# Four matmuls to a weight load in a cached-attention decode kernel: K in groups of eight pairs with the transposes by halves of the head, V in four PSUM banks for two pairs, w_down behind the last K

## Chip, cores, metric

One core of a Trainium2 chip runs the kernel. The metric is the device time of one execution in microseconds (us). All runs told here are of the state "fast"; the program has one core, so there is no second die to disturb it.

## The reference, cut to what matters

```python
# A_: attention of one new token against a cache; B_: a gated MLP on the same batch (its own w_gate, w_up, w_down)
x: (4, 1, 1024)   k_cache, v_cache: (4, 32, 8192, 128)   wq: (1024, 4096)   wo: (4096, 1024)     # all bf16
q = (x @ wq) per head;  p = softmax(q . k_cache / sqrt(128));  o = p . v_cache;  a = o @ wo
b = x + sigmoid(r) * ((silu(x @ w_gate) * (x @ w_up)) @ w_down)          # w_*: 1024 x 3584 and 3584 x 1024
out = g * a + (1 - g) * b
```

The two caches are 537 MB, everything together 575.7 MB, read once.

## The kernel before

K and V are walked in 32 *pairs* (four heads of one batch row, 8 MB of K or of V each; the name is the program's, for two ring slots of 4 MB). A ring of five slots in SBUF takes all large loads in program order. For K, VectorE (DVE) transposes 32x32 blocks of 32-bit words and TensorE (PE) multiplies by a shifted copy of q, so that all scores of a group of pairs collect in one PSUM tile. After a group comes a softmax; then V of the group is multiplied by the weights, a pair of V after each pair of K. At the end several V pairs follow each other without K between them, and the blocks of w_o come last.

```python
CJ = 32; JT = 4; RD = 8; GD = 4        # 8 transposes a pair, 4 pairs a group
LAG = GD                               # V runs one group behind K
ring = const.tile([P, NS, RING], BF)   # NS = 5 slots of 4 MB
...
def k_pair(d):
    ks = load_pair(kv_view(A_k_cache, d), RING)
    for n in range(RD):
        nc.vector.transpose(out=flat_t, in_=kn[:, c * CJ * Dh:(c + 1) * CJ * Dh])           # 128x2048 words
        for he in range(4):
            for z in range(2):                                                              # 2 matmuls a load
                nc.tensor.matmul(sps[:, z, :], lhsT=Z[:, he, s:s + P], rhs=T[:, 16*z:16*z+16, half, :, e], ...)
        ...
def v_pair(d):
    for c, z, w:                                                                            # cut
        for e in range(2):                                                                  # 2 matmuls a load
            nc.tensor.matmul(o_ps[row:row + NM, e, :], lhsT=PB[:, RD * t + c, z, w], rhs=vn[...], ...)
    if t < GD - 1:
        return
    nc.scalar.activation(out=o_sb, in_=o_ps[:, 0, :], func=ACT.Copy, scale=mE[:, 0:1])       # "OS": once in 4 pairs
    nc.vector.scalar_tensor_tensor(out=o_sb, in0=o_ps[:, 1, :], scalar=mE[:, 1:2], in1=o_sb, ...)
    ...                                   # later: 4 small matmuls pick the rest out of o_sb
...
last = [wo_block(g) for g in range(2, NWB - 2)] + ...   # w_o: blocks 0, 1 before the last V pair, 2 to 7 behind it
last.pop(0)()                             # block 2
flush(); flush_late()                     # the last OS goes through its small matmuls
last.pop(0)()                             # block 3
o_rows(GE, NWB)                           # rows of w_o blocks 4 to 7 (GE = 4)
for use in last: use()
```

## Time and profile before

| | before |
|---|---|
| time, median of the first 3 runs (range) | 1343.87 us (1343.86 to 1344.13) |
| PE, DVE busy | 77%, 46% |
| weight loads of K and V | 2048, about 206 us, beside the matmuls |
| DMA | 575.69 MB, 99.5% busy, 429 GB/s |

The page of the kernel before, busy us of each engine (share of the span) and number of instructions. Besides PE and DVE it names PEld (PE's weight loads), ACT (ScalarE) and POOL (GpSimd); SP, further down, is the engine that issues most DMAs:

```profile
PE 1032.8 (77%) x4552; PEld 227.9 (17%) x2364; DVE 614.4 (46%) x369; ACT 50.6 (4%) x46; POOL 62.8 (5%) x161
```

The DMA view of the kernel before: totals, the large queue (packets, MB, share of 16 engines' span), and two lines of the issue table (size of one DMA, median us from issue to landing; the second group, with no size, holds several sizes).

```profile
DMA packets 14316, 576.18 MB, mean 429 GB/s; under 512 B 1598, under 2 KB 1606, under 8 KB 2252
q1 hardware_dynamic: 14276, 575.69, 99.5%
...
ring<-in_A_k_cache_dram SPq DMA_DIRECT2D x14, 4096.0 KB, 34.1
...
ring<-in_A_k_cache_dram SPq DMA_DIRECT2D x25, 36.2
```

The loads are nearly never idle. The issue table says how much is queued ahead: a DMA that takes much longer from issue to landing than its own bytes need stands behind others.

The groups of instructions of the kernel before (busy us, mean ns of one, then the idle time before them and what ended it): transposes, weight loads of K and V, and the two instructions of the OS step.

```profile
L436 DVE STREAM_TRANSPOSE TB<-ring 128x2048 uint32<-128x2048 uint32 x256 | 566.9, 2277 | 492.4 <-DMA ring<-in_A_k_cache_dram 491.5 <-PE S_ps L442 0.8
L442 PEld LDWEIGHTS <-Z 128*128 128x128 bf16 x1024 | 105.4, 103 | 628.0 <-issue 626.4
L513 PEld LDWEIGHTS <-PB 128*32 128x32 bf16 x1024 | 100.7, 98 | 405.1 <-issue 393.7 <-POOL PB L486 5.2 <-POOL Z L421 0.9
L526 DVE SCALAR_TENSOR_TENSOR OS<-o_ps,mE,OS 128x512 f32<-128x512 f32 x8 | 6.0, 751 | 72.2 <-ACT OS L525 72.2
L525 ACT ACTIVATE OS<-o_ps,mE 128x512 f32<-128x512 f32 x8 | 5.5, 687 | 162.8 <-PE o_ps L513 162.8
```

The chain that ended last, in order of time, for the last 82 us of the kernel before (start us, us, what). It goes from V's matmuls back onto the DMA: from 1290 us the end waits for data.

```profile
1260.90 2.81 PE o_ps L513 x8
1263.71 1.82 PE small L533 x8
1265.53 24.73 PE o_ps L513 x112
...
1290.27 30.99 DMA ring<-in_A_v_cache_dram
...
1321.33 16.11 DMA ring<-in_A_wo_dram
...
1337.47 1.90 PE acc L273 x8
```

At 1260.90 the fourth last V pair (pair 28) begins. From there to the end of the span (1342.2) are 81.3 us (*stretch from pair 28 on*).

### The profile page before, as it was taken

Reading aid. Unit: us, or ns where it says so; the run is one execution under the profiler, and the core shown is the slowest. Engines: PE = TensorE matmul, PEld = TensorE weight load, DVE = VectorE, ACT = ScalarE, POOL = GpSimd, SP = SyncE. Lnnn points to the kernel's source line nnn. Section 1 sums busy time; section 2 is a strip of 40 time slices with the busy share of each in tenths; the row PEclk is TensorE's granted clock in tenths of the full one; section 3 lists DMA queues with packets and bytes.
Section 4 is the critical chain, followed back from the end, with each engine's and each line's share of the span. In section 5 each row is a group of like instructions: output and inputs, shape, how many; then the busy total and the mean of one; then the engine's idle time right before and its main releaser. Section 6 shows DMA issues by size and latency. Waiting matters only on the chain.

```text
span 1342.2 us, 7696 instructions
## 1 busy us (share of the span) xinstructions
PE 1032.8 (77%) x4552; PEld 227.9 (17%) x2364; DVE 614.4 (46%) x369; ACT 50.6 (4%) x46; POOL 62.8 (5%) x161
## 2 busy tenths in 40 slices
PE   2565878787788687778977779597778679877898
PEld 0111111111111121111211112111111112111221
DVE  2555655545336554335455556046555254556000
ACT  0000100001000010001000010000100010000100
POOL 2000100001000010001000010000100010000100
PEclk9787988888998888889988889888889899888899
DMA  9999999999999999999999999999999999999997
GB/s 414 436 432 431 439 434 427 445 430 422 445 424 430 442 432 426 438 434 428 438 436 426 432 430 434 436 433 438 428 423 436 430 431 442 436 419 444 419 425 325
DMA packets 14316, 576.18 MB, mean 429 GB/s; under 512 B 1598, under 2 KB 1606, under 8 KB 2252
## 3 DMA queue, kind: packets, MB, share of 16 engines
q1 hardware_dynamic: 14276, 575.69, 99.5%
q8 instruction: 27, 0.44, 0.1%
q14 instruction: 5, 0.04, 0.0%
q10 hardware_dynamic: 8, 0.00, 0.0%
HBM read 575.68 MB, written 0.01 MB: 429 GB/s over the span
## 4 chain that ended last, share of the span: by engine, by line
DMA 66%; DVE 21%; PE 11%; another core or an unknown queue 1%; ACT 0%; issue 0%; SPq 0%; DVEq 0%
DMA ring<-in_A_k_cache_dram 58%; DVE TB L436 21%; PE o_ps L513 9%; DMA ring<-in_A_v_cache_dram 5%; DMA x<-in_gate_w_dram 2%; DMA ring<-in_A_wo_dram 1%; PE S_ps L442 1%; ACT PB L484 0%; PE S_ps L307 0%; PE acc L307 0%; PE acc L273 0%; PE small L533 0%; ACT OS L525 0%; PE small L472 0%
## 5 line engine op out<-in xcount | busy, mean ns | idle before, releaser
L436 DVE STREAM_TRANSPOSE TB<-ring 128x2048 uint32<-128x2048 uint32 x256 | 566.9, 2277 | 492.4 <-DMA ring<-in_A_k_cache_dram 491.5
L442 PE MATMUL S_ps<-TB,Z 128*128 128x512 bf16 x2048 | 518.8, 408 | 219.4 <-DVE TB L436 218.9
L513 PE MATMUL o_ps<-ring,PB 128*32 128x512 bf16 x2048 | 461.4, 388 | 52.6 <-DMA ring<-in_A_v_cache_dram 48.1
L442 PEld LDWEIGHTS <-Z 128*128 128x128 bf16 x1024 | 105.4, 103 | 628.0 <-issue 626.4
L513 PEld LDWEIGHTS <-PB 128*32 128x32 bf16 x1024 | 100.7, 98 | 405.1 <-issue 393.7
L421 POOL COPY Z<-qa 32x4 bf16<-32x4 bf16 x128 | 25.6, 200 | 761.6 <-PE S_ps L442 736.0
L486 POOL COPY PB<-PT 32x1024 bf16<-32x1024 bf16 x16 | 30.3, 1892 | 430.3 <-PE o_ps L513 426.2
L467 ACT ACTIVATE PTs<-S_ps,mx 128x1024 bf16<-128x1024 f32 x8 | 8.9, 1114 | 1020.9 <-DVE mx L463 1020.9
L526 DVE SCALAR_TENSOR_TENSOR OS<-o_ps,mE,OS 128x512 f32<-128x512 f32 x8 | 6.0, 751 | 72.2 <-ACT OS L525 72.2
L484 ACT COPY PB<-PT 32x1024 bf16<-32x1024 bf16 x16 | 30.5, 1908 | 1.5 <-DVE PT L469 1.3
L474 DVE RECIPROCAL rinv<-small 128x16 f32<-128x16 f32 x8 | 2.1, 258 | 42.0 <-PE small L472 42.0
L370 DVE CAST LT<-small 128x64 bf16<-128x64 f32 x2 | 0.4, 224 | 42.3 <-PE small L368 42.3
L236 PE MATMUL small<-identb,x 6*128 6x6 bf16 x8 | 0.6, 195 | 22.3 <-DMA x<-in_gate_w_dram 22.3
L457 DVE TENSOR_REDUCE mx<-S_ps 128x1 f32<-128x1024 f32 x8 | 9.8, 1225 | 15.9 <-PE S_ps L442 15.9
L273 PE MATMUL acc<-ring,LT 128*4 128x512 bf16 x64 | 14.8, 379 | 1.7 <-DMA ring<-in_A_wo_dram 1.0
L469 DVE STREAM_TRANSPOSE PT<-PTs 128x1024 bf16<-128x1024 bf16 x8 | 10.0, 1245 | 10.2 <-ACT PTs L467 10.2
L273 PE MATMUL acc<-ring,hT 128*4 128x512 bf16 x56 | 12.2, 379 | 0.0
L525 ACT ACTIVATE OS<-o_ps,mE 128x512 f32<-128x512 f32 x8 | 5.5, 687 | 162.8 <-PE o_ps L513 162.8
L307 PE MATMUL o_ps<-ring,xw 128*4 128x512 bf16 x56 | 5.7, 536 | 5.3 <-DMA ring<-in_B_w_gate_dram 5.3
L533 PEld LDWEIGHTS small<-selg,OS 128*128 128x128 f32 x64 | 9.0, 208 | 4.1 <-issue 3.9
L533 PE MATMUL small<-selg,OS 128*128 128x16 f32 x64 | 8.7, 269 | 0.0
L238 DVE COPY xw<-small 128x48 bf16<-128x48 bf16 x1 | 0.2, 181 | 15.9 <-PE small L236 15.9
(64 smaller groups left out, 67.2 us busy)
## 6 DMA issues: line engine op xcount, KB each, us to landing
ring<-in_A_k_cache_dram SPq DMA_DIRECT2D x14, 4096.0 KB, 34.1
ring<-in_A_v_cache_dram SPq DMA_DIRECT2D x14, 4096.0 KB, 31.4
ring<-in_B_w_gate_dram SPq DMA_DIRECT2D x1, 7168.0 KB, 37.1
ring<-in_B_w_up_dram SPq DMA_DIRECT2D x1, 7168.0 KB, 39.2
ring<-in_B_w_down_dram SPq DMA_DIRECT2D x2, 3584.0 KB, 27.4
ring<-in_A_wo_dram SPq DMA_DIRECT2D x6, 1024.0 KB, 24.7
ring<-in_A_v_cache_dram SPq DMA_DIRECT2D x2, 2048.0 KB, 28.7
ring<-in_A_v_cache_dram SPq DMA_DIRECT2D x4, 1024.0 KB, 24.7
```

The source lines that it names most:

```text
L273: nc.tensor.matmul(out_ap, lhsT=lhsT, rhs=rhs, start=start, stop=True, skip_group_check=True)
L421: nc.gpsimd.tensor_copy(out=Z[at, :, QP - 1 + QP * q], in_=qa[at, :, h0 + q, b])
L436: nc.vector.transpose(out=flat_t.bitcast(U32), in_=kn[:, c * CJ * Dh:(c + 1) * CJ * Dh].bitcast(U32))
L442: nc.tensor.matmul(sps[:, z, :], lhsT=Z[:, he, s:s + P], rhs=T[:, 16 * z:16 * z + 16, half, :, e], start=(t == 0 and n == 0 and he == 0), ...
L457: nc.vector.tensor_reduce(out=mx[:, 0:1], in_=sps[:].rearrange("p z n -> p (z n)"), axis=AX.X, op=ALU.max)
L467: nc.scalar.activation(out=PTs[:], in_=sps[:].rearrange("p z n -> p (z n)"), func=ACT.Exp, bias=negm[:, 0:1], scale=scale, accum_out=rs[:, ...
L469: nc.vector.transpose(out=PT[:].rearrange("p j i -> p (j i)"), in_=PTs[:])
L484: nc.scalar.copy(out=Bv[at, :, :, q, :], in_=Pv[at])
L486: nc.gpsimd.tensor_copy(out=Bv[at, :, :, q, :], in_=Pv[at])
L513: nc.tensor.matmul(o_ps[row:row + NM, e, :], lhsT=PB[:, RD * t + c, z, w].rearrange("p e s j -> p (e s j)"), rhs=vn[:, j0 * Dh:(j0 + 4) * ...
L526: nc.vector.scalar_tensor_tensor(out=o_sb[:], in0=o_ps[:, 1, :], scalar=mE[:, 1:2], in1=o_sb[:], op0=ALU.mult, op1=ALU.add)
L533: nc.tensor.matmul(oT[:, :], lhsT=o_sb[:, q * Dh:(q + 1) * Dh], rhs=selg[:, q].rearrange("p t s -> p (t s)"), start=(q == 0), stop=(q == 3))
```

## The change

Its intent: a weight load for every four matmuls, no longer for every two. For K, a transpose takes 64 rows of one half of the head (strided input), so that four PSUM banks are filled from one load; the group has eight pairs. For V, four banks collect two pairs. K and V now take four banks each, and the program leaves none for anything else: the diff drops the pool of small tiles and the accumulator of two banks. Three things follow. The small results share banks. w_down, which collected in its own banks from early on, moves behind the last K. And V's banks have to be emptied after every second pair by a new step, the *sums*: a multiply by a mask (`own` in the code) out of PSUM and a reduction of 16 parts on DVE (16 times, in place of the OS step 8 times).

```diff
-    CJ = 32
+    CJ = 64                                # RD = 4, GD = 8
+    GV = 2
 ...                                       # k_pair
-            nc.vector.transpose(out=flat_t.bitcast(U32), in_=kn[:, c * CJ * Dh:(c + 1) * CJ * Dh].bitcast(U32))
-            for he in range(4):
-                for z in range(2):
+            for half in range(2):
+                nc.vector.transpose(out=..., in_=kn[:, half].bitcast(U32))
+                for e in range(2):
+                    for z in range(4):
+                        nc.tensor.matmul(sps[:, z, :], lhsT=Z[:, 2 * half + e, s:s + P], rhs=T[:, 16 * z:16 * z + 16, :, e], ...)
+                step = 2 * n + half
+                if step == 1:
+                    flush_sums()
 ...                                       # v_pair
+        flush_sums()
 ...
+        for u in range(4 * RD):
+            for w in range(4):
+                nc.tensor.matmul(o_ps[row:row + NM, w, :], lhsT=PB[:, ...], rhs=vn[...], ...)
 ...
-        nc.scalar.activation(out=o_sb[:], in_=o_ps[:, 0, :], func=ACT.Copy, scale=mE[:, 0:1])
-        nc.vector.scalar_tensor_tensor(out=o_sb[:], in0=o_ps[:, 1, :], ...)
+        def sums():
+            kept = turned(P, 16 * Dh, F32)
+            nc.vector.tensor_tensor(out=kept..., in0=o_ps[:]..., in1=own[:]..., op=ALU.mult)
+            nc.vector.tensor_reduce(out=OS[:], in_=kept.rearrange("p (k d) -> p d k", d=Dh), axis=AX.X, op=ALU.add)
+        full.append(sums)
 ...                                       # order of work
-    side = {1: lambda: (gu_piece(B_w_up, 1), h_done()), GD - 1: wd_piece}
+    side = {1: lambda: (gu_piece(B_w_up, 1), h_done())}
+            if d == ND - 1:
+                A_ps.append(scp.tile([P, 4, NB], F32, name="S_ps"))
+                wd_piece()
+                add_x()
 ...                                       # after the last V pair: blocks 2, 3, the last sums, 4, rows of 6 and 7, 5, 6, 7
+    flush_sums()
```

## The prediction

> **What bounds the kernel now.** DMA. The page's queue table: 575.69 MB on one queue, busy for 99.5% of the span, mean 429 GB/s. In stretches of 10 us the DMA share is about 1 from the first on (never under 0.89) and falls only in the last 10 us. The Trainium skill, "DMA: Bandwidth & Descriptors", Specifications, gives a ceiling of 435 GB/s; this trace's 429, head and tail included, is 98.6% of it. At 435 the bytes need 1323 us (estimate from that page), so no change to compute can take off more than some 12 us. Compute is behind the data: PE is busy 77%, DVE 46%; K's transposes were preceded by 491.5 us of idle ended by DMA. A K pair takes 36.2 us from issue to landing (issue table), though its 8 MB move in about 19.5 us: some 17 us of other data is still queued ahead, so a consumer may be about that late before the queue runs dry.
>
> **What the change removes.** Half the weight loads of K and V: 1024 of 2048, at 103 and 98 ns, about 103 us of PEld. They are hidden already: in V stretches of the chain 64 matmuls take 13.93 us, 217 ns each, with a load for every second one. The skill, "TensorE: Matmul & The Clock Gate", on LDWEIGHTS, says that loads are pulled ahead of running matmuls; the trace agrees. A few ns per matmul at most come back, and PE is not the limit. Matmuls and their columns stay, and so do the 256 transposes of 2277 ns, if the strided input costs no more.
>
> **What it adds and moves.** Sixteen pairs of DVE instructions (multiply 128x2048 out of PSUM, reduce 128x2048) for eight ACT/DVE pairs of 0.69 + 0.75 us. From the trace's 1.22 us per 1024 elements I estimate 2.3 us each, 74 us in all; DVE busy goes from 614 to about 680 us. A delay of 4.6 us every second pair is inside 17 us. The softmax is half as often and twice as wide, a stall of some 8 us, also inside. The first stretch becomes eight K pairs without V; DVE needs 17.66 us per pair against 19.5 of DMA. w_down (7 MB, 12.2 us of PE) moves to the end, where V needs 14 us of PE per 19.5 us of DMA.
>
> **The tail.** After the last V piece (1325.7 us) the OS step takes 3.2 us longer, but its rows are needed two w_o blocks (3.8 us) later. The end is still the last w_o landing (1337.4), 1.9 us of matmuls, a copy and the store: -1 to +3 us.
>
> **Predicted time:** 1344.5 us; 8 in 10 between 1340.5 and 1348.5. Faster by over 2%: 0.01; within 2%: 0.95; slower by over 2%: 0.04.
>
> **What would show it.** PEld instructions of K and V halve, PEld busy falls by some 100 us; DVE rises by 60 to 80 us; the mean rate stays at 428 to 431 GB/s, the DMA share about 1 in every stretch; the chain still goes back mostly through DMA.
>
> **What would make it wrong.** K transposes well over 2.45 us each through the strided input (the K stretch would starve the queue); a strided reduction of twice my 2.3 us (+2 us in the tail); matmuls waiting for the shared PSUM banks so long that slots come free over 17 us late; a DMA share clearly under 1 mid-run.

## The result, and the profile after

| | before | after |
|---|---|---|
| median of 6 runs (range) | 1343.88 us (1343.76 to 1344.14) | 1349.70 us (1346.55 to 1352.53) |
| ratio, 95% interval | | 1.0042 (1.0029 to 1.0055) |
| granted clock of the profiled run | 0.902 | 0.903 |
| stretch from pair 28 on | 81.3 us | 85.8 us |
| last w_o piece landed, from the span's start | 1338.7 us | 1343.0 us |
| span | 1342.2 us | 1350.4 us |

A ratio is the mean time of one kernel's fast runs over that of the other's of the same rounds, so not quite the ratio of the medians. The change is slower by 0.4%, clear of the noise, within 2%, and outside the range predicted. The profiled run is the slowest of the six.

The page and then the DMA view, after:

```profile
PE 1060.8 (79%) x4512; PEld 128.6 (10%) x1300; DVE 697.8 (52%) x370; ACT 44.5 (3%) x30; POOL 62.8 (5%) x161
```

```profile
DMA packets 14311, 576.10 MB, mean 427 GB/s; under 512 B 1598, under 2 KB 1606, under 8 KB 2252
q1 hardware_dynamic: 14276, 575.69, 99.2%
...
ring<-in_A_k_cache_dram SPq DMA_DIRECT2D x14, 4096.0 KB, 29.8
```

The groups after. Loads are halved, transposes unchanged, and the sums are new:

```profile
L454 DVE STREAM_TRANSPOSE TB<-ring 128x2048 uint32<-128x2048 uint32 x256 | 568.1, 2278 | 436.4 <-DMA ring<-in_A_k_cache_dram 415.2 <-PE S_ps L457 21.2
L548 DVE TENSOR_REDUCE OS<-TB 128x128 f32<-128x2048 f32 x16 | 57.9, 3618 | 0.5
L529 PEld LDWEIGHTS <-PB 128*64 128x64 bf16 x512 | 57.5, 112 | 432.4 <-issue 420.1 <-POOL PB L502 10.9 <-DMA ring<-in_A_v_cache_dram 0.9
L457 PEld LDWEIGHTS <-Z 128*128 128x128 bf16 x512 | 53.7, 105 | 684.0 <-issue 684.0
L546 DVE TENSOR_TENSOR TB<-o_ps,own 128x2048 f32<-128x2048 f32 x16 | 36.3, 2267 | 133.5 <-PE o_ps L529 133.4
```

The weight-load time fell by 99 us and bought nothing on PE: 64 matmuls of V take 13.93 us before (a load for every second one) and 13.93 us after (for every fourth). The reduction costs 3.62 us, where 2.3 had been estimated.

The chain that ended last, after, from pair 28 on. The DMA is gone from it; PE, the multiply (TB L546), the reduction (OS L548) and PE again follow each other to the end.

```profile
1264.61 3.59 PE o_ps L529 x8
...
1268.73 25.17 PE o_ps L529 x120
...
1293.92 2.30 DVE TB L546
...
1296.24 3.63 DVE OS L548
...
1300.51 13.77 PE o_ps L529 x56
...
1318.57 13.95 PE o_ps L529 x64
...
1332.53 2.30 DVE TB L546
...
1334.86 3.62 DVE OS L548
...
1341.60 5.35 PE S_ps L284 x24
```

PE's own timeline for two spots of this stretch (start, us, what, count; in brackets the idle time before it and what ended it): pair 30 cannot write the banks before the multiply has read them (2.38 us), then waits for the reduction; at the end PE waits 2.48 us for the last reduction and only then can go on to the last rows of w_o. The stop at pair 30 also costs more than its own length: the eight matmuls behind it take 3.07 us, where eight without a stop take 1.89. The granted clock between 1295 and 1300 us was 0.68 here and 0.54 in the control below, against 1.00 in the kernel before.

```profile
1296.26 3.07 PE L529 MATMUL o_ps<-ring,PB 128*64 128x512 bf16 x8 [2.38 <-DVE TB L546]
1299.92 0.59 PE L554 MATMUL S_ps<-sel,OS 128*128 128x8 f32 x2 [0.59 <-DVE OS L548]
...
1338.52 0.39 PE L554 MATMUL S_ps<-sel,OS 128*128 128x8 f32 x2 [2.48 <-DVE OS L548]
```

The last w_o piece had landed at 1343.0, and 7.4 us passed to the end of the span; before it was 3.5 us. So one part of the loss lies in the tail. Another part lies in the middle, for that piece itself landed 4.3 us later than before, although the bytes are the same. The chain shows where, in one of several like spots:

```profile
355.02 33.14 DMA ring<-in_A_k_cache_dram
...
388.25 4.50 DVE TB L454 x2
392.75 2.19 DVE TB L546
...
394.96 3.63 DVE OS L548
398.59 4.42 DVE TB L454 x2
...
403.03 24.45 DMA ring<-in_A_k_cache_dram
```

Two transposes, then the sums (5.8 us), then two transposes, and only then is a slot free and the next K pair issued, at 403.03. It lands after 24.45 us. The very first load of this size, into an empty queue, took 22.0 us. So there was almost nothing queued ahead: the queue nearly ran dry (I call this a *drain*). In the packet records of the trace, 64 KiB packets mostly take 2.42 us; at such a spot a dozen or more take 3 us or so (*slowed packets*). Between 20 and 1200 us the kernel before has 25 of 6016 such packets over 2.6 us, the changed kernel has 133 of 5871. The loss stands mostly in these packets and not in an idle queue. From 3 us to the last w_o landing the 16 DMA engines were idle for 2.8 us on average, against 2.0 before; what the slowed packets took over 2.42 us, shared among 16 engines, is 4.9 us, against 0.8 before (an estimate from the packet records). Together that is 4.9 us more than before, near the 4.3 us between the two landings.

### The profile page after: what moved, and what is told of

It is laid out like the page before. It is cut to its first block, busy times and chain, and to the rows that moved or that the text cites. A ratio compares the mean times of both kernels' runs of the same rounds, so it can differ in the third digit from the quotient of the medians.

```text
span 1350.4 us, 6579 instructions
## 1 busy us (share of the span) xinstructions
PE 1060.8 (79%) x4512; PEld 128.6 (10%) x1300; DVE 697.8 (52%) x370; ACT 44.5 (3%) x30; POOL 62.8 (5%) x161
## 4 chain that ended last, share of the span: by engine, by line
DMA 53%; DVE 27%; PE 17%; another core or an unknown queue 1%; issue 1%; ACT 0%; SPq 0%; DVEq 0%
DMA ring<-in_A_k_cache_dram 47%; DVE TB L454 20%; PE o_ps L529 12%; DMA ring<-in_A_v_cache_dram 4%; DVE OS L548 4%; PE S_ps L457 3%; DVE TB L546 2%; PE S_ps L284 2%; DMA x<-in_gate_w_dram 2%; DVE mx L475 0%; ACT TB L485 0%; PE S_ps L318 0%; DVE PT L487 0%; PE S_ps L554 0%
## 5 line engine op out<-in xcount | busy, mean ns | idle before, releaser
L454 DVE STREAM_TRANSPOSE TB<-ring 128x2048 uint32<-128x2048 uint32 x256 | 568.1, 2278 | 436.4 <-DMA ring<-in_A_k_cache_dram 415.2
L457 PE MATMUL S_ps<-TB,Z 128*128 128x512 bf16 x2048 | 543.0, 419 | 209.3 <-DVE TB L454 209.0
L529 PE MATMUL o_ps<-ring,PB 128*64 128x512 bf16 x2048 | 465.8, 390 | 32.7 <-DMA ring<-in_A_v_cache_dram 24.0
L457 PEld LDWEIGHTS <-Z 128*128 128x128 bf16 x512 | 53.7, 105 | 684.0 <-issue 684.0
L546 DVE TENSOR_TENSOR TB<-o_ps,own 128x2048 f32<-128x2048 f32 x16 | 36.3, 2267 | 133.5 <-PE o_ps L529 133.4
L529 PEld LDWEIGHTS <-PB 128*64 128x64 bf16 x512 | 57.5, 112 | 432.4 <-issue 420.1
L548 DVE TENSOR_REDUCE OS<-TB 128x128 f32<-128x2048 f32 x16 | 57.9, 3618 | 0.5
L284 PE MATMUL S_ps<-ring,hT 128*4 128x512 bf16 x56 | 14.7, 431 | 5.4 <-ACT TB L485 5.4
L284 PE MATMUL S_ps<-ring,LT 128*4 128x512 bf16 x64 | 14.5, 379 | 1.1 <-DVE LT L381 0.7
L487 DVE STREAM_TRANSPOSE PT<-TB 128x2048 bf16<-128x2048 bf16 x4 | 9.2, 2311 | 8.5 <-ACT TB L485 8.5
L475 DVE TENSOR_REDUCE mx<-S_ps 128x1 f32<-128x2048 f32 x4 | 9.2, 2292 | 8.2 <-PE S_ps L457 8.2
```

Of the source, the lines that this page charges most:

```text
L284: nc.tensor.matmul(acc(n), lhsT=lhsT, rhs=rhs, start=start, stop=True, skip_group_check=True)
L454: nc.vector.transpose(out=flat_t.bitcast(U32).rearrange("p (j i) -> p j i", j=CJ), in_=kn[:, half].bitcast(U32))
L457: nc.tensor.matmul(sps[:, z, :], lhsT=Z[:, 2 * half + e, s:s + P], rhs=T[:, 16 * z:16 * z + 16, :, e], start=(t + n + half + e == 0), stop ...
L475: nc.vector.tensor_reduce(out=mx[:, 0:1], in_=sps[:].rearrange("p z n -> p (z n)"), axis=AX.X, op=ALU.max)
L487: nc.vector.transpose(out=PT[:].rearrange("p j i -> p (j i)"), in_=PTs)
L529: nc.tensor.matmul(o_ps[row:row + NM, w, :], lhsT=PB[:, RD * (t % (GD // 2)) + n, z].rearrange("p w s j -> p (w s j)"), rhs=vn[:, j0 * Dh: ...
```

## The experiments

Theories. **D**: the sums hold up the transposes that free K's slots, the DMA queue runs dry or nearly so, and the middle loses. **P**: from pair 28 on the tail is one chain of PE work and of PE's waits for the sums; it no longer ends with the DMA. Rivals: the longer groups and shared banks (R), w_down's matmuls behind the last K (T2).

The texts of the expectations say "fifth last" for V pair 27, "fourth last" for 28, and so on. Each run was timed in five rounds (4 to 6 fast timings each) against the kernel before on the same chip. e5, e6 and e10 ran on a second chip and e11 on a third, so their comparison with the control crosses chips; the kernel before was within 0.15 us on all three.

| run | edit | median us (range) | stretch from pair 28 | last w_o landed | landing to end |
|---|---|---|---|---|---|
| a0_after | none (control) | 1348.69 (1346.98 to 1352.61) | 86.0 | 1338.5 | 7.8 |
| e1_sums_first | sums before K's transposes | 1348.75 (1347.36 to 1349.76) | 86.1 | 1339.0 | 8.8 |
| e2_reduce_twice | reduction done twice | 1381.28 (1379.42 to 1383.20) | 98.8 | 1359.3 | 20.3 |
| e3_few_wd_matmuls | 52 of 56 w_down matmuls left out | 1348.50 (1347.06 to 1353.46) | 86.2 | 1342.1 | 9.0 |
| e4_no_last_reduce | last reduction 1/16 | 1346.91 (1345.76 to 1349.84) | 84.0 | 1339.5 | 5.6 |
| e11_tail_reduces_short | last three reductions 1/16 | 1345.86 (1344.79 to 1347.63) | 81.7 | 1339.3 | 4.2 |
| e6_pe_sums | cheaper sums | 1344.86 (1344.61 to 1345.29) | 82.0 | 1338.7 | 4.1 |
| e7_pe_sums_first | cheaper sums, before K's transposes | 1344.62 (1344.48 to 1345.49) | 82.4 | 1339.6 | 4.1 |
| e10_contiguous_reduce | stride moved to the multiply | 1350.57 (1347.25 to 1353.52) | 85.9 | 1340.7 | 7.4 |
| e5_before_delay | kernel before, sums' cost in K alone | 1344.33 (1343.83 to 1345.32) | 79.6 | 1339.8 | 3.5 |
| e8_wo_before_v30 | w_o blocks 0, 1 one pair earlier | 1354.50 (1354.28 to 1356.86) | 92.6 | 1338.8 | 13.9 |
| e9_all_three | e7 and e8 together | 1354.12 (1353.97 to 1355.17) | 92.5 | 1338.7 | 14.7 |

The kernel before took 1343.87 to 1344.02 (medians). The last three columns are from the profiled run of each. The stretch from pair 28 on measures PE's chain only where the end waits for PE. Where the DMA sets the end (the kernel before, e5, e6, e7, nearly e11), a later start of pair 28 makes it shorter: in e5 pair 28 begins 2.8 us later than in the kernel before. There "landing to end" is the better guide.

### a0_after: the control

> The changed kernel again, as a control on the same chip as the next three. Expected 1349 us with a spread of several us (its six runs went from 1346.6 to 1352.5), against 1343.9 for the kernel before.

It came as expected, with the same wide spread; its ratio to before is 1.0039 (1.0027 to 1.0051). Its profiled run was one of the faster: 84 slowed packets where the first profile had 133, the last w_o piece at 1338.5 us as in the kernel before, and still 7.8 us from there to the end. So the tail's loss is there even when the middle loses nothing.

### e1_sums_first: the sums out of K's way

```diff
+        flush_sums()
         for n in range(RD):
 ...
-                if step == 1:
-                    flush_sums()
```

> The sums (multiply and reduce, 5.9 us on DVE) run before a K pair's first transpose, where DVE waits for data anyway, instead of between its transposes. Theory D (the sums hold up the transposes that free K's slots, and the DMA queue runs dry for a moment in the middle of the run): the slowed packets and short idle spots in the middle go, the last w_o piece lands 3 to 4.5 us earlier (near 1339 from the span's start), the total falls to about 1345.5 us. Rival R (the longer groups, the doubled softmax or the shared PSUM banks make the slots late, or the DMA is slower for another reason): the total stays within 1 us of the control.

DVE's timeline in this run shows that the move worked: the sums now stand ahead of a pair's transposes.

```profile
305.76 2.29 DVE L545 TENSOR_TENSOR TB<-o_ps,own 128x2048 f32<-128x2048 f32 x1 [15.98 <-PE o_ps L528]
308.08 3.58 DVE L547 TENSOR_REDUCE OS<-TB 128x128 f32<-128x2048 f32 x1
311.58 15.46 DVE L455 STREAM_TRANSPOSE TB<-ring 128x2048 uint32<-128x2048 uint32 x7
```

The slowed packets went (32 between 20 and 1200 us, against 84 of the control and 25 before). The median did not: 1348.75 against 1348.69. By the total this is the outcome that I had given to rival R, and D missed; R is settled further down, by e6 and e7. What changed is the spread: the slowest run is 1349.76, against 1352.61. So it is shown that the sums between the transposes make the slowed packets, but my size for them (about 4 us) was that of an unlucky run. In the mean of the runs e1 is 0.5 us under its control, which is not clear of the noise.

### e2_reduce_twice: the dose doubled

```diff
             nc.vector.tensor_reduce(out=OS[:], in_=kept..., axis=AX.X, op=ALU.add)
+            nc.vector.tensor_reduce(out=OS[:], in_=kept..., axis=AX.X, op=ALU.add)
```

> The reduction of the sums is done twice in place (same result): 3.6 us more of DVE per second pair. Theory D: the slack in the queue is used up, so each of some 12 to 16 sums costs most of its 3.6 us more: plus 20 to 50 us in the middle and plus 3.6 us in the tail, total 1372 to 1400 us. Rival R: plus 3.6 us in the tail alone, total about 1353 us.

It took 32.6 us more than the control, in the range of D. In stretches of 10 us (the last three numbers are PE's granted clock, DMA share and GB/s) the queue now clearly runs dry; first this run, then the changed kernel as profiled first:

```profile
400.00:410.00 10.00, 5.45 (x15) 0.39 (x3) 10.00 (x5) 0.00 (x0) 0.00 (x0) 0.55 0.78 315
800.00:810.00 10.00, 8.29 (x32) 1.07 (x9) 10.00 (x5) 0.00 (x0) 0.00 (x0) 0.75 0.80 315
```

```profile
400.00:410.00 10.00, 9.14 (x32) 1.12 (x9) 10.00 (x7) 0.00 (x0) 0.00 (x0) 0.70 1.01 400
800.00:810.00 10.00, 10.00 (x48) 1.42 (x13) 3.83 (x3) 0.00 (x0) 0.78 (x4) 1.00 0.98 419
```

The last w_o piece landed 20.8 us later than in the control, and the stretch from pair 28 on grew by 12.8 us (three sums lie on it). Both mechanisms answer to the length of the sums. My reading, from these two runs: the 5.9 us of the change stand just at the edge of the queue's slack, and 3.6 us more fall over it.

### e3_few_wd_matmuls: is it w_down?

```diff
-        for i in range(FG * FR):
+        for i in (0, NR):
```

> Wrong result on purpose: w_down is loaded as before, but only 4 of its 56 matmuls are done (one row of each half). It takes some 13 us of PE away from behind the last K. Theory T1 (the tail is late through the sums after the last V, PE having met the DMA again at the fifth last V pair, where it waits 4.7 us): no gain, within 1 us of the control. Rival T2 (w_down's matmuls behind the last K make PE late to the end): 2.5 to 4 us faster.

The result is wrong. The median is 1348.50, the stretch from pair 28 on 86.2 us: no gain. PE had simply waited longer for the next V pair (8.5 us). T2 falls: moving w_down behind the last K costs nothing that these runs show, as had been predicted.

### e4_no_last_reduce and e11_tail_reduces_short: the sums in the tail

```diff
-            nc.vector.tensor_reduce(out=OS[:], in_=kept..., axis=AX.X, op=ALU.add)
+            kd = kept.rearrange("p (k d) -> p d k", d=Dh)
+            nc.vector.tensor_reduce(out=OS[:], in_=kd if d < ND - 1 else kd[:, :, 0:1], ...)     # e4
+            nc.vector.tensor_reduce(out=OS[:], in_=kd if d < ND - 5 else kd[:, :, 0:1], ...)     # e11
```

> Wrong result on purpose: the reduction after the last V pair takes one of its 16 parts only, so 3.4 us of DVE leave the end of the chain. Theory P (from the fifth last V pair's end on the tail is one chain of PE work and of PE's waits for the sums, 86.0 us long from the first matmul of the fourth last V pair to the end in all four changed variants seen, whatever the DMA does, against 81.3 before): PE's wait of 2.5 us for the last sums goes, 2 to 2.5 us faster than the control's 1348.7 to 1349.4, and that stretch becomes about 83.5 us. Rival (the end is set by the last DMA): no change.

> Wrong result on purpose: the last three reductions (those after the fifth last, third last and last V pairs) take one part of 16 only; the thirteen in the middle keep their 3.6 us. If the tail makes nearly all of the loss, the stretch from the fourth last V pair's first matmul to the end falls from 86.0 to about 82.5 to 83 us and the median to 1345.5 to 1346.5 us, with some runs up to 3 us more from the drains in the middle, which stay. If the drains in the middle make most of it, it stays above 1347 us.

Both results are numerically wrong; the comparison with the reference let both pass, so it does not see such a loss. e4 took 1.8 us less than the control of the call before, the stretch went from 86.0 to 84.0: the direction of theory P, a little under the 2 to 2.5 us expected. Its ratio to before is 1.0026 (1.0013 to 1.0040), which overlaps the control's; the wait itself is gone. e11 took 2.8 us less than that control, ratio 1.0018 (1.0005 to 1.0032); the stretch is 81.7 us, 0.4 us longer than before the change. PE's timeline in e11: only the multiply is still waited for, and the last block of w_o waits for its data again.

```profile
1293.49 2.98 PE L529 MATMUL o_ps<-ring,PB 128*64 128x512 bf16 x8 [2.38 <-DVE TB L546]
...
1338.04 1.89 PE L284 MATMUL S_ps<-ring,LT 128*4 128x512 bf16 x8 [0.15 <-DMA ring<-in_A_wo_dram]
```

So three reductions in the tail hold about 3 us of the 4.8 to 5.8 us, with the thirteen sums in the middle left as they are. (The stretch fell by 4.3 us and the total by less, for in e11's profiled run pair 28 began 1.5 us later than in the control's.) Some of e11's runs are still 2 us slower than its fastest; the drains in the middle are still there (89 slowed packets).

### e6_pe_sums and e7_pe_sums_first: cheaper sums

```diff
-    OS = const.tile([P, Dh], F32)
+    OS = const.tile([P, 8 * Dh], BF)
+    selb = ...                                                                         # sel in bf16
 ...
-            kept = turned(P, 16 * Dh, F32)
+            kept = turned(P, 16 * Dh)                                              # bf16
-            nc.vector.tensor_reduce(out=OS[:], in_=kept..., axis=AX.X, op=ALU.add)
+            nc.vector.tensor_tensor(out=OS[:], in0=kept[:, 0:8 * Dh], in1=kept[:, 8 * Dh:16 * Dh], op=ALU.add)
 ...
-            nc.tensor.matmul(oT, lhsT=OS[:], rhs=sel[:]..., start=True, stop=True, ...)
+            for k in range(8):
+                nc.tensor.matmul(oT, lhsT=OS[:, k * Dh:(k + 1) * Dh], rhs=selb[:]..., start=(k == 0), stop=(k == 7), ...)
```

e7 has in addition the edit of e1.

> The sums in bf16, 8 of 16 parts left to be added by eight matmuls in place of the strided reduction, and done before a K pair's transposes: DVE 3 us in place of 5.9. Theory P: the last wait of 2.5 us and the drains in the middle go, the wait for the multiply stays: 1345.5 to 1346.5 us, the stretch from the fourth last V pair on about 83.5 us. If it equals the control, theory P is wrong on the last wait.

> The cheaper sums (bf16, an add of halves, eight matmuls in place of the strided reduction) where the change has its sums, after two of a K pair's transposes. Theory P: the last wait is gone and DVE is held 3 us in place of 5.9, so nothing is left of the drains: 1344.5 to 1345.5 us, within 0.5 us of the same with the sums first (1344.6). Theory D: 1 us or more slower than that one.

e7 came out a little better than expected: 1344.62, ratio to before 1.0006 (0.9993 to 1.0018). e6 is 1344.86, 1.0006 (0.9994 to 1.0019): where the sums stand does not matter once they are short. Both keep the groups of eight pairs, the shared banks and w_down's new place. So rival R, and T2 with it, can hold little more than the 0.6 to 0.8 us that are left (2.5 us at the upper end of the intervals). The chain of e7 ends with the DMA again, as before the change:

```profile
1290.25 31.88 DMA ring<-in_A_v_cache_dram
...
1322.19 16.11 DMA ring<-in_A_wo_dram
...
1338.33 1.90 PE S_ps L286 x8
```

The 1.3 us between the means of e11 and e6 I put down to the sums in the middle, which e11 leaves long; this is not shown, for the intervals overlap and the chips differ. The spread of the runs shrinks with them from 2.8 us (e11) to 0.7 (e6).

### e10_contiguous_reduce: is it the stride?

```diff
-            nc.vector.tensor_tensor(out=kept.rearrange("p (k d) -> p k d", d=Dh), in0=o_ps..., ...)
-            nc.vector.tensor_reduce(out=OS[:], in_=kept.rearrange("p (k d) -> p d k", d=Dh), ...)
+            nc.vector.tensor_tensor(out=kept.rearrange("p (d k) -> p k d", d=Dh), in0=o_ps..., ...)
+            nc.vector.tensor_reduce(out=OS[:], in_=kept.rearrange("p (d k) -> p d k", d=Dh), ...)
```

> The multiply writes its product with the 16 parts side by side, so that the reduction reads in sequence. If the stride makes the reduction 3.62 us, it falls to about 2.3 us (the maximum over 128x2048 took 2.29) and the multiply stays near 2.27 or grows; with 1.3 us saved in the last wait the total is 1 to 1.5 us below the control, near 1347.5 us. If the reduction stays at 3.6 us, the stride is not its cost and the total stays.

The groups of this run:

```profile
L546 DVE TENSOR_TENSOR TB<-o_ps,own 128x2048 f32<-128x2048 f32 x16 | 57.0, 3565 | 132.5 <-PE o_ps L529 132.4
L548 DVE TENSOR_REDUCE OS<-TB 128x128 f32<-128x2048 f32 x16 | 36.6, 2286 | 0.6
```

The stride is the cost, and it moved: the reduction fell to 2.29 us and the multiply, which now writes with a stride, rose to 3.57 us. The sum is 5.85 us in place of 5.89, and the time did not fall (1350.57). I had expected a saving of 1 to 1.5 us; the reduction fell as expected, but the rise of the multiply took the saving back. The Trainium skill, "SBUF — State Buffer", the note on SBUF "cachelines", says that accesses which cross to a new 16-byte line each time pay a penalty; this case agrees, at 1.3 us for 2048 float32 elements per partition, reading 512 bytes apart or writing 64 bytes apart.

### e5_before_delay: the cost in the middle alone

```diff
 # in the kernel before, in k_pair
+            if n == 1 and d > LAG and (d - LAG) % 2 == 0:
+                kept = turned(P, 16 * Dh, F32)
+                nc.vector.tensor_tensor(out=kept, in0=kept, in1=kept, op=ALU.mult)
+                nc.vector.tensor_reduce(out=extra[:], in_=kept.rearrange("p (k d) -> p d k", d=Dh), axis=AX.X, op=ALU.add)
```

> The kernel before with one part of the change's cost alone: in every second K pair from the seventh on (13 in all) a multiply 128x2048 and a strided reduction of 128x2048 (some 5.9 us of DVE, results thrown away) stand after the second transpose; nothing is added to the V tail. If delays between K's transposes made most of the loss (theory D), plus 2 to 5 us. If the tail makes it (theory P), 1344 to 1345 us, within 1 us of the kernel before.

1344.33, ratio 1.0003 (0.9989 to 1.0017). Thirteen delays of 5.9 us between K's transposes are nearly free in the kernel before, although they too brought slowed packets (90). This agrees with e1: the middle is not where most of the loss is.

### e8_wo_before_v30 and e9_all_three: an attempt that failed, and was wrong

```diff
-        if (kind, d) == ("v", ND - 1):
+        if (kind, d) == ("v", ND - 2):
+            o_rows(0, 4)
             for g in range(2):
                 wo_block(g)()
 ...
-            o_rows(0, GE)
+            o_rows(4, GE)
```

> The first two w_o blocks (16 matmuls, with the copy of their rows some 4.4 us of PE) move from before the last V pair to before the one but last, where PE otherwise waits 2.4 us for the multiply and 0.7 us for the reduction of the sums and then starts at a lower clock. Theory P: the waits are covered, the stretch from the fourth last V pair's first matmul to the end shrinks by 3 to 4.5 us to about 82 us, total 1345 to 1346. Rival (end set by DMA, or PE's work behind the last K): no change.

> Cheaper sums, before K's transposes, and the two w_o blocks moved. Theory P: PE no longer binds the tail, the end is set by the last w_o landing as in the kernel before: 1343.5 to 1344.5 us, equal to the kernel before within 1 us and not better, for the bytes set the time.

e8 was 5.8 us slower than the control and e9 9.5 us slower than e7, on which it was built, against the expectation. The wait for the multiply before pair 30 was covered, as meant (PE waited 1.23 us there, for data), but PE then stood before the w_o blocks behind the last V pair. In the timeline of e8, first SP, which issues the last nine loads of w_o over 36.08 us (25.07 in the control), then PE:

```profile
1294.07 36.08 SPq L391 DMA_DIRECT2D ring<-in_A_wo_dram  x9
...
1335.11 5.74 PE L284 MATMUL S_ps<-ring,LT 128*4 128x512 bf16 x16 [8.01 <-DMA ring<-in_A_wo_dram]
```

The last piece had landed at 1338.8 as ever. PE has its work in fixed order, and 8.0 us of it was pushed behind that. The kernel's code and the trace settle why. w_o's blocks 0 to 3 share one slot of the ring and blocks 4 to 7 another, each taken at the first of its blocks. With blocks 0 and 1 moved before pair 30, the two last V pairs take the other four of the five slots, so that the slot of blocks 4 to 7 is the slot of blocks 0 to 3. The loads of blocks 6 and 7 then go where blocks 2 and 3 lie. They were issued from 1326.39 us on, just after block 2 had landed (1326.33), and PE's matmuls for blocks 2 and 3 waited until 1335.07 and later for the semaphores of these loads; e9 shows the same waits. So blocks 2 and 3 were computed with the weights of 6 and 7: the results of e8 and e9 are wrong, and the comparison, which does not see such a loss either, passed them. As tests of the move the two runs are void. They say nothing against P (the waits that it names did go), and they don't confirm its 3 to 4.5 us either.

## Why the prediction was wrong

Right:

- The bytes bind. In eight of the twelve variants the last w_o piece lands 1338.5 to 1339.6 us from the start, in the kernel before at 1338.7. The kernel before moves 429 GB/s of the 435 that the Trainium skill, "DMA: Bandwidth & Descriptors", Specifications, gives as ceiling. No variant beat the kernel before, and no experiment pointed to one that would. (The prediction's limit of some 12 us does not follow from its figures, 1342.2 less 1323 is 19; nothing rests on it.)
- Halved weight loads buy nothing: PEld fell by 99 us, and 64 matmuls still take 13.93 us. The skill, "TensorE: Matmul & The Clock Gate", on the LDWEIGHTS step, says that loads are pulled ahead of running matmuls; the trace agrees.
- The strided transposes cost the same (2277 and 2278 ns), and w_down at the end costs nothing that shows (e3).
- DVE rose by 83 us. I said 60 to 80; the reduction alone is 16 times 1.3 us over the estimate. The mean rate came out at 427 GB/s, just under the 428 to 431 predicted.

Wrong. The step that failed, as the prediction put it: "After the last V piece (1325.7 us) the OS step takes 3.2 us longer, but its rows are needed two w_o blocks (3.8 us) later. The end is still the last w_o landing". (The 1325.7 us is when PE's last V matmul ended; the last V piece had landed at 1323.8.) In its place the runs showed that the end is no longer the landing, but a chain of PE and of its waits for the sums, 7.4 to 7.8 us past the landing where it was 3.5:

1. *A term mis-sized.* The reduction takes 3.62 us, not 2.3, for its input is strided (e10). The OS step is 5.9 us in place of 1.45, so 4.5 us longer and not 3.2. The prediction had named a slow strided reduction as a risk, but at +2 us. It also set only the increase (3.2 us) against the 3.8 us of w_o work; the whole step, 4.6 us by its own figures, already exceeds them, and the measured one left PE waiting 2.48 us.
2. *A wait left out.* In the tail V pairs follow each other, so the next pair cannot write the four banks before the multiply has read them, and its small matmuls wait for the reduction (2.4 and 0.6 to 0.7 us at pair 30), and the first eight matmuls after the wait take 2.9 to 3.1 us in place of 1.89. With four banks for two pairs there is no second set to go on in. I had set 14 us of PE against 19.5 us of DMA per pair and called it room enough, without adding these stops and the eight w_o blocks. In the kernel before, PE's last V matmul ended 1.9 us after the last V piece had landed; in the changed one 4.5 to 4.9 us after. So PE came late to the last OS step as well.
3. Together these make the stretch from pair 28 on 86.0 us in place of 81.3: 4.7 us. e4 takes 2.0 us of it away, e11 4.3 us, both by shortening nothing but reductions in the tail. An estimate from the control's trace divides the loss: its last V matmul ends at 1328.4 us, the sums take 6.0 us to PE's next matmul, and 11.9 us of work follow. With 1325.7 for 1328.4 and 4.7 for 6.0, as predicted, the chain would end near 1342.3, where the kernel before ended (1342.2). So of the 4.1 us that this run lost, about 2.7 are the stops left out and about 1.3 the mis-sized reduction.

A second step was half wrong: "A delay of 4.6 us every second pair is inside 17 us". The 17 us came from a median of issue-to-landing times. The queue's slack is set by its smallest: of the 8 MB loads whose landing the trace tells, the shortest took 27.4 us in the kernel before and 24.3 in the changed one, where an empty queue gives 22.0. By this measure the slack was some 5 us before the change, not 17 (an estimate). The slots came late often enough for the queue nearly to run dry (133 slowed packets), and in e2 quite (16 us of idle queue and 32.6 us of time). In the runs of the change this is worth from nothing to about 4 us. In the mean it may be 0.5 us (e1 against its control) to 1.3 us (e6 against e11); neither is clear of the noise. It seems to make a good part of the spread (5.6 us in the control, 2.4 in e1).

What stays open: the cheaper sums are still 0.6 to 0.8 us above the kernel before, an interval that includes zero; and how the loss of a single run divides between tail and middle, since only one run of each kernel has a trace. Why packets are slowed when the queue is nearly empty is not known, nor whether the w_o blocks can be moved without the clash of slots.

## What to carry to other kernels

When a kernel is bound by DMA, saved work on a hidden engine is worth nothing, but new work is not free: ask where the engine has no other stage to hide behind, above all in the tail, and add up all its stops there, also those where it waits for a bank to be emptied. Take the slack of a load queue from the shortest time between issue and landing, not the median, and compare it with that of a load into an empty queue. Before spreading an accumulator over all banks, cost the step that empties it, stride included, at every place where it stands on the chain. And when loads change their order in a ring, count the slots again: a comparison that passes does not show that the data was right (e8).

## What the Trainium skill lacked or had wrong

- "TensorE: Matmul & The Clock Gate", Back-to-back issue gap: it gives a sustained 131 ns per matmul at N=512 and calls the 216 ns of its formula for an isolated matmul gap too high for a pipelined stream. Here long streams of 128x512 bf16 matmuls take 217 ns each (64 in 13.93 us), with a load for every second or every fourth alike. The formula is what holds.
- "DMA: Bandwidth & Descriptors", Specifications: the row "HBM-per-NC limit ~358 GB/s" stands there without its condition (the page tells it further down: both cores of the pair streaming). One core alone reads 429 GB/s here over a whole kernel.
- "SBUF — State Buffer", the "cachelines" note: it has no figure for DVE. Here a stride costs 1.3 us per 2048 float32 per partition, on the reading side (3.62 against 2.29 us) or on the writing side (3.57 against 2.27 us) alike.
- No page that I read has it: a queue that runs dry costs more than the gap, for the first 64 KiB packets afterwards take some 3 us in place of 2.42 (2.8 to 3.5 us in e2 at 407 and 804 us; so do the first packets of the kernel before).
